# A planned order for VectorE's chains, weight conversions held behind a chain, and one product group in eight products

## The chip, the core and the metric

One core of a Trainium2 chip runs the whole program: TensorE (PE, with its weight loads PEld), VectorE (DVE), ScalarE (ACT), GpSimd (POOL) and SyncE (SP), the last two mostly issuing DMA. The metric is the device time of one execution in microseconds. Before the change the median of three executions is 723.2 us (722.88 to 724.81).

## The reference, cut to what matters

A gated recurrence with complex gates per head, then a dense block with squared relu:

```python
mag = np.sqrt(a_re * a_re + a_im * a_im)
scale = np.minimum(mag, 0.999) / (mag + 1e-06)
a_re_n, a_im_n = (a_re * scale, a_im * scale)
for t in range(S):                      # S = 768; batch 4, 8 heads, head_dim 48
    new_re = ar * S_re - ai * S_im
    new_im = ar * S_im + ai * S_re
    kv = np.einsum('bhd,bhe->bhde', k[:, :, t], v[:, :, t])
    S_re, S_im = (new_re + kv, new_im)
    y[:, :, t] = np.einsum('bhd,bhde->bhe', q[:, :, t], S_re)
...
h = x @ w_in                            # x: 3072 x 384, w_in: 384 x 2048
r = np.maximum(h, 0.0)
return ((r * r) @ w_out).astype(np.float32)   # w_out: 2048 x 384
```

## The kernel before, in words

The 3072 rows are worked in six **units** of 512 rows. For each unit there are three stages.

The **chain** (function `chain`) turns the gates of the unit into running products. A unit's heads are held in two halves of four heads (z = 0 and 1, tiles `aq0`, `f0` and `aq1`, `f1`). For each half `roots` and `normalise` bring the gates to the right length: ScalarE does squares, Ln and Exp (L905 to L917), VectorE L901 to L929. `inner` multiplies four neighbouring rows together: three rounds of two products (L948) and two sums (L954, L956), each round needing the one before. TensorE then turns the last products (L981, tile `xn`), ScalarE copies them to `e` (L996 to L1005), and `scan` runs through them on VectorE: a long row of small complex products, each two multiplications and a sum (L1031, L1033, L1035), ending in `xn` (L1094, L1099). That is turned back (L981, L1116). `apply` multiplies the result into the gates (L1165, L1169), takes the magnitude (L1173 to L1185) and forms the products with k and q (L1188, L1197) that the next stage reads; `gather` moves the k products by DMA to the tile `KC` (L1233).

The **pairs** (function `pairs`) work on two heads at a time, four pairs to a unit. In units 0 and 1 TensorE transposes (L1292) and ScalarE copies (L1296, tile `QT`); later units transpose on VectorE and by DMA. TensorE forms the scores (L1310), VectorE masks them (L1313, tile `A`), TensorE forms the states from the gathered tile (L1338), VectorE sums these (L1347, L1349), TensorE multiplies scores and states with v and q (L1362, L1366, bank `yp`), ScalarE copies the result (L1372) and a DMA puts it into `xT`.

The **dense** stage (function `dense`) works a unit in two groups of 256 rows: hidden blocks on TensorE (L1402), relu and square on ScalarE (L1433, L1434), and the projection. Unit 0 projects with the plain product (L1448). Later units use either `eight` (eight products of half size, L1499) or `seven` (seven products with sums of operands made on VectorE at L1514 and sums of results at L1523). The list `SEVEN` says which; before, these are the second groups of units 1 and 2 and both groups of units 3 to 5. The sums of weights that `seven` needs are made at L1489.

The **weights** arrive as 64-bit numbers in 16 pieces, 8 of each matrix, and are converted on the chip: for each piece ScalarE scales the low words (L795), VectorE masks and shifts the high words (L801), carries the top bits (L805) and adds (L808). In a piece that is `mixed` ScalarE does the top bits in another way (L799), and L805 is not there. Pieces 0 to 5 of the first matrix and the last two pieces of the second are not mixed before. Raw pieces wait in tiles that are not yet needed (`raw1`, `raw2`), two of them in the `g` tile and three in the room of the second matrix.

The order of all instructions comes from the class `Plan`. Each step names its engine, an assumed duration, the keys it reads and writes, and a rank. `order` is a list scheduler: of the engine that can start first it takes, among the steps that are ready, the one of lowest rank. Ranks are pairs: matmuls' followers (0, n), pairs (1, n), chain (2, n) with small offsets, conversions (2, 0.3) and (2, 0.6), dense (3, n), checks of the weights (5, ...). A step is ready when its producers are done plus a hop per engine; a producer on the same engine has no hop. The result is written out engine by engine, and each engine runs its list in that order and waits where it must. A step may hold several instructions: two of the recurrence's products, all three of a complex product.

`check` steps are range checks: sums of squares of q, k, v and the gates, and maxima, that decide at the end whether a slower general path has to run. They are ScalarE squares with an accumulated sum (L932, L936, L1138, L1141).

## Time and profile before

| what | value |
|---|---|
| median of three executions | 723.2 us |
| the profiled execution | 726.46 us |
| its span, first to last instruction | 724.7 us |
| granted TensorE clock, mean | 0.985 |
| PE busy | 637.5 us (88%) |
| DVE busy | 555.9 us (77%) |
| ACT busy | 354.9 us (49%) |
| POOL busy | 176.2 us (24%) |
| DMA | 79.51 MB, mean 110 GB/s |

The profile is of one execution. A busy share is a mean over stages with different limits. In unit 0 there is no dense work yet, so TensorE is idle and the chain is seen bare; later units' chains run beside the dense work of the unit before. Names such as `f<-aq` say which tile an instruction writes and which it reads. A row of the timeline gives the start, the duration, the engine, the line, the operation and how many were merged. A wait is put down to what came last. Some matmul records are missing from the trace, so a short hole of TensorE put down to "issue" need not be idle time.

### The profile page before, as it was taken

The page shows a single profiled execution, that of the slowest core. Times are in us where ns is not written, and L with a number is a line of the kernel's source. Part 1 is how long each engine was busy: PE and PEld are TensorE (multiplying, and loading weights), DVE is VectorE, ACT ScalarE, POOL GpSimd, SP SyncE. Part 2 cuts the span into 40 slices and gives each one's busy share as a digit, 9 for nine tenths or more (in the row PEclk, how much of TensorE's full clock was granted, in tenths as well). Part 3 has the DMA queues.
Part 4 walks back from the last instruction along what each step waited for, and adds up shares of the span by engine and source line. Part 5 has one row for each costly group of instructions (what it writes and reads, how often), then busy time and mean ns, then how long its engine had stood idle before and what let it go on. Part 6 is the DMA issues. An engine that isn't in the chain of part 4 may idle for free. (4 is left out here: it accounts for less than half of the span.)

```text
span 724.7 us, 11426 instructions
## 1 busy us (share of the span) xinstructions
PE 637.5 (88%) x4042; PEld 570.8 (79%) x4042; DVE 555.9 (77%) x1125; ACT 354.9 (49%) x588; POOL 176.2 (24%) x334
## 2 busy tenths in 40 slices
PE   0005779999999999986999999999999999999996
PEld 0005668678768998985998898999998989989996
DVE  6999995798878597977796587897887979428721
ACT  6674456958475435324824556535448344032230
POOL 6502427051400003305022432022223033023200
PEclk9999989999999999998999999999999999999998
DMA  9730348530441003456016555016543043358600
GB/s 287 240 125 22 98 107 177 209 66 18 133 129 30 1 23 100 114 158 152 2 30 167 146 124 103 1 33 164 133 147 73 0 120 78 94 191 326 239 2 27
DMA packets 56355, 79.51 MB, mean 110 GB/s; under 512 B 10944, under 2 KB 38464, under 8 KB 56288
## 3 DMA queue, kind: packets, MB, share of 16 engines
q0 software_dynamic: 15232, 40.72, 18.2%
q1 hardware_dynamic: 36928, 32.98, 18.1%
q10 hardware_dynamic: 4128, 4.98, 2.5%
q8 instruction: 34, 0.56, 0.3%
q14 instruction: 33, 0.27, 0.1%
HBM read 48.76 MB, written 4.72 MB: 74 GB/s over the span
## 5 line engine op out<-in xcount | busy, mean ns | idle before, releaser
L1402 PE MATMUL d<-xT,w 128*128 128x256 f32 x1056 | 238.4, 383 | 4.9 <-issue 3.5
L1402 PEld LDWEIGHTS d<-xT,w 128*128 128x128 f32 x1056 | 199.5, 191 | 33.7 <-issue 5.9
L1499 PE MATMUL d<-w,g 128*128 128x192 f32 x768 | 131.9, 327 | 0.0
L1499 PEld LDWEIGHTS d<-w,g 128*128 128x128 f32 x768 | 125.2, 190 | 0.7 <-issue 0.4
L1233 POOL DMA_DIRECT2D KC<-f x160 | 79.1, 502 | 154.7 <-DVE f L1197 91.7
L1433 ACT ACTIVATE g<-d 128x512 f32<-128x512 f32 x88 | 52.2, 593 | 106.2 <-PE d L1402 83.9
L1460 POOL DMA_DIRECT2D out_dram<-ot x22 | 12.3, 559 | 244.6 <-DVE ot L1523 184.7
L1499 PE MATMUL d<-T,g 128*128 128x192 f32 x384 | 68.0, 327 | 0.0
L1499 PEld LDWEIGHTS d<-T,g 128*128 128x128 f32 x384 | 62.7, 190 | 0.6 <-issue 0.6
L1434 ACT ACTIVATE g<-g 128x512 f32<-128x512 f32 x96 | 60.5, 631 | 3.0
L1372 ACT COPY yt<-yp 112x512 f32<-112x512 f32 x24 | 26.4, 1101 | 72.0 <-PE yp L1366 66.1
L1514 DVE TENSOR_TENSOR g<-g 128x512 f32<-128x512 f32 x64 | 42.9, 683 | 24.0 <-ACT g L1434 14.0
L875 POOL DMA_DIRECT2D v<-in_v_dram x80 | 46.3, 586 | 48.2 <-ACT ot L1518 19.6
L1310 PE MATMUL sc<-QT 96*128 96x128 f32 x368 | 48.5, 286 | 3.7 <-ACT QT L1296 2.3
L1310 PEld LDWEIGHTS sc<-QT 96*128 96x128 f32 x368 | 44.9, 198 | 6.8 <-ACT QT L1296 3.4
L1165 DVE TENSOR_TENSOR f<-aq,xn 128x384 f32<-128x384 f32 (+1 forms) x64 | 45.4, 751 | 1.4 <-ACT xn L1116 1.3
L1197 DVE TENSOR_TENSOR f<-aq 128x384 f32<-128x384 f32 (+1 forms) x64 | 45.0, 753 | 0.5
L1448 PE MATMUL d<-w,g 128*128 128x384 f32 x128 | 43.6, 488 | 0.0
L1362 PE MATMUL yp<-A,v 128*48 128x128 f32 x320 | 36.1, 299 | 3.7 <-DVE A L1313 3.6
L948 DVE TENSOR_TENSOR f<-aq 128x384 f32<-128x384 f32 x72 | 36.9, 554 | 1.0
L1313 DVE TENSOR_TENSOR A<-sc,mask 128x512 f32<-128x512 f32 x45 | 30.0, 684 | 8.2 <-PE sc L1310 8.0
L1523 DVE TENSOR_TENSOR ot<-ot,d 128x192 f32<-128x192 f32 x64 | 21.7, 349 | 19.0 <-PE d L1499 18.6
(186 smaller groups left out, 944.9 us busy)
## 6 DMA issues: line engine op xcount, KB each, us to landing
QT<-aq SPq DMA_DIRECT2D x128, 64.0 KB, 2.0
f<-in_moe_w_in_dram POOLq DMA_DIRECT2D x8, 768.0 KB, 7.0
f<-in_moe_w_out_dram POOLq DMA_DIRECT2D x8, 768.0 KB, 6.4
KC<-f POOLq DMA_DIRECT2D x104, 48.0 KB, 1.8
out_dram<-ot POOLq DMA_DIRECT2D x22, 192.0 KB, 2.4
QT<-aq ACTq DMA_DIRECT2D x64, 64.0 KB, 2.3
v<-in_v_dram POOLq DMA_DIRECT2D x80, 48.0 KB, 3.5
xT<-yt SPq DMA_DIRECT2D x36, 96.0 KB, 2.4
```

The lines of the kernel that those rows point to most:

```text
L875: lambda i=i, c=c, src=src: pool.dma_start(out=t[32 * c:32 * c + 32, i], in_=src[c]), vrank, 32 * 1536, 4.0,
L948: dve.tensor_tensor(out=f, in0=a[:, :, :, c - 1], in1=a[:, j, :, c].unsqueeze(1).to_broadcast([C, 2, HH, D]), op=ALU.mult)
L1165: lambda j=j, r=r: dve.tensor_tensor(out=f4[:, j, r], in0=a[:, r], in1=over(j), op=ALU.mult), late[z])
L1197: lambda j=j, r=r, o=o: dve.tensor_tensor(out=o[:, :, :, r * D:(r + 1) * D], in0=qk[:, j], in1=a[:, r], op=ALU.mult), late[z])
L1233: lambda i=i, c=c, queue=queue: queue.dma_start(out=kc[32 * c:32 * c + 32, i], in_=nat[32 * i:32 * i + 32, c]),
L1310: pe.matmul(sa[:, j], lhsT=T[:, j, 1, h], rhs=T[:, j, 0, h], start=True, stop=True)
L1402: pe.matmul(ps, lhsT=w1[:, f // FP, m, ts(f % FP, C)], rhs=xT[:, n % 2, m, ts(grp, G)], start=(m == 0), stop=(m == NM - 1))
L1433: act.activation(out=o, in_=ps, func=AF.Relu)
L1434: act.activation(out=o, in_=o, func=AF.Square)
L1448: pe.matmul(ps, lhsT=gt[:, f % 2, ts(i, C)], rhs=w2[:, f], start=(f == 0), stop=(f == NF - 1))
L1499: pe.matmul(bank[b][:, 0:DH], lhsT=g4[:, r, j], rhs=w(j), start=first and j == 0, stop=last and j == NT - 1)
L1514: step("DVE", tt(4 * C), gk(x0, h) + gk(x1, h), gk(o, h), lambda: dve.tensor_tensor(out=g4[:, o, sl], in0=g4[:, x0, sl], in1=g4[:, x1, sl] ...
```

## The change

It changes the planner's rules, cuts steps finer, and moves some work. Line numbers of the new file differ from those of the profile; where rows of the new order are shown, the words beside them give the old line.

- *Distance behind the producer.* A producer on the same engine whose result is read now counts with a hop (`DRAIN`: 0.12 us on VectorE, 0.13 on ScalarE). Steps of several instructions are cut into single ones: the recurrence's products and sums, each complex product of the scan, the copies and sign changes beside it.
- *Holding for the chain.* When the best ready step has a rank of (2, 0.2) or more, which includes conversions, the planner looks ahead (`HOLD`: 0.15 us on VectorE, 0.8 on ScalarE) and takes a step of lower rank that will be ready by then.
- *Unit 0's roots* get a rank ahead of its recurrence.
- *Pairs' products unlinked.* In `apply` the two halves of a complex product get keys of their own, and the product with k is written to a scratch tile in place of over k, so that the steps behind wait for less.
- *Five weight pieces later.* Pieces 3 to 7 of the first matrix are converted behind unit 0's pairs in the plan, held until the recurrence of its second half is done. Pieces 3, 4 and 5 become `mixed`: their three L805 go, three L799 come. The tiles of the raw pieces change places: pieces 1 and 2 now wait in `g`, 3 to 5 in the second matrix's room.
- *Range checks.* One square of the roots now accumulates its own sum in place of a second square; the checks of q, k and v get a rank of (2, n + 0.9), behind the unit's chain.
- *Seven and eight.* The second group of unit 1 uses `eight`.
- Assumed durations on ScalarE: 0.08 us less for each, 0.22 more for one that accumulates.

The core of the diff:

```diff
+    HOLD, URGENT, FILL = {"DVE": 0.15, "ACT": 0.8}, (2, 0.2), (2, 0.2)
+    DRAIN = {"DVE": 0.12, "ACT": 0.13}
...
-                hop = 0.0 if same else self.HOP[steps[d][0]]
+                hop = self.HOP[steps[d][0]]
+                if same:
+                    hop = self.DRAIN.get(e, 0.0) if d in steps[n][7] else 0.0
...
+            if steps[n][4] >= self.FILL and e in self.HOLD:
+                m = min((m for m in wait[e] if at[m] <= t + self.HOLD[e]),
+                        key=lambda m: (steps[m][4], m))
+                if steps[m][4] < self.URGENT:
+                    n, t = m, max(t, at[m])
...
+    SOON = 3
...
-    SEVEN = [(n, grp) for n in range(FAST, NU) for grp in range(n < 3, 2)]
+    SEVEN = [(n, grp) for n in range(FAST, NU) for grp in range(n < 3, 2) if n > 1]
...
-        return n / 1200.0 + 0.18
-
+        return n / 1200.0 + 0.10
+
+    SUM = 0.22
...
+    raw1 = [(KC[1].bitcast(U32), [("KC", 1, 0), ("KC", 1, 1)])] + graw + [w2slot(s) for s in (2, 1, 0)]
...
+        held = [("a", 1)] if SOON <= i < NPIECE else []
...
-        mixed = NPIECE - 2 <= i < 2 * NPIECE - 2
+        mixed = SOON <= i < 2 * NPIECE - 2
...
-        step("DVE", ts2(PW), keys, wk, lambda: dve.tensor_scalar(
+        step("DVE", ts2(PW), keys + held, wk, lambda: dve.tensor_scalar(
...
-        first = (CHAIN, 0.25) if n == 1 else rank
+        first = (CHAIN, 0.25) if n == 1 else (CHAIN, n - 0.02) if n == 0 else rank
...
+            check("ACT", ac(Y) + SUM, key(z, 1), key(z, 3), lambda: act.activation(
+                out=t, in_=f1, func=AF.Square, accum_out=sums[:, n, 2 + z:3 + z]), first)
...
-            check("ACT", ac(Y), key(z, 3), [], lambda: act.activation(
-                out=junk[:, 0:Y], in_=t, func=AF.Square, saturate=False,
-                accum_out=sums[:, n, 2 + z:3 + z]), first)
...
-                step("DVE", 2 * tt(m) + 0.06, [("a", z)], key(z, 0), lambda c=c: terms(c), ahead)
-                step("DVE", 2 * tt(m // 2) + 0.06, key(z, 0), [("a", z)],
-                     lambda c=c: joined(c), ahead)
+                for j in range(2):
+                    step("DVE", tt(m), [("a", z)], [("in", z, j)] + (key(z, 0) if c == 1 else []),
+                         lambda c=c, j=j: dve.tensor_tensor(
+                             out=f[j], in0=a[:, :, :, c - 1],
+                             in1=a[:, j, :, c].unsqueeze(1).to_broadcast([C, 2, HH, D]),
+                             op=ALU.mult), ahead)
+                for r, op in ((0, ALU.subtract), (1, ALU.add)):
+                    step("DVE", tt(m // 2), [("in", z, 0), ("in", z, 1)] + key(z, 0), [("a", z)],
+                         lambda c=c, r=r, op=op: dve.tensor_tensor(
+                             out=a[:, r, :, c], in0=f[0][:, r], in1=f[1][:, 1 - r], op=op), ahead)
...
-            def go():
-                dve.tensor_tensor(out=g1, in0=xx, in1=y(0, 1).to_broadcast(shape),
-                                  op=ALU.mult)
-                dve.tensor_tensor(out=g2, in0=xx[:, ::-1], in1=y(1, 3)[:, ::-1],
-                                  op=ALU.mult)
-                dve.tensor_tensor(out=dst, in0=g1, in1=g2, op=ALU.add)
-            step("DVE", 3 * tt(cnt) + 0.24, reads, writes + (own or K), go, rk)
+            for i, (g, x_, y_) in enumerate(((g1, xx, y(0, 1)), (g2, xx[:, ::-1], y(1, 3)[:, ::-1]))):
+                step("DVE", tt(cnt), reads, [(own, i)],
+                     lambda g=g, x_=x_, y_=y_: dve.tensor_tensor(
+                         out=g, in0=x_, in1=y_.to_broadcast(shape), op=ALU.mult), rk)
+            step("DVE", tt(cnt), [(own, 0), (own, 1)], writes,
+                 lambda: dve.tensor_tensor(out=dst, in0=g1, in1=g2, op=ALU.add), rk)
...
-                check("ACT", ac(Y), [("qk", j)] + [("k", j)] * r, [], lambda r=r: act.activation(
+                check("ACT", ac(Y) + SUM, [("qk", j)], [], lambda r=r: act.activation(
                     out=junk, in_=QK[j][:, ts(r, Y)], func=AF.Square, saturate=False,
-                    accum_out=sums[:, n, 4 + 2 * j + r:5 + 2 * j + r]), late[j])
-            check("ACT", ac(Y), [("v", vs(n))], [], lambda: act.activation(
+                    accum_out=sums[:, n, 4 + 2 * j + r:5 + 2 * j + r]), (CHAIN, n + 0.9))
+            check("ACT", ac(Y) + SUM, [("v", vs(n))], [], lambda: act.activation(
                 out=junk, in_=vv[vs(n)][:, ts(j, Y)], func=AF.Square, saturate=False,
-                accum_out=sums[:, n, 8 + j:9 + j]), late[1])
+                accum_out=sums[:, n, 8 + j:9 + j]), (CHAIN, n + 0.9))
...
-                step("DVE", tt(n1), kf[0] + kf[1], [("a", z)],
+                step("DVE", tt(n1), kf[0] + kf[1] + [("a", z)], [("ap", z, p, r)],
...
-            step("DVE", tt(n1), kf[1] + [("qk", z)], [("k", z)],
+            step("DVE", tt(n1) + 0.06, kf[1] + [("qk", z)], kf[0],
                  lambda: dve.scalar_tensor_tensor(
-                     out=qk[:, 1].rearrange("p h c d -> p (h c d)"), in0=t,
-                     scalar=lv[:, n, 1:2], in1=qk[:, 1].rearrange("p h c d -> p (h c d)"),
+                     out=f0, in0=t, scalar=lv[:, n, 1:2],
+                     in1=qk[:, 1].rearrange("p h c d -> p (h c d)"),
...
-            for i in range(NPIECE):
+            for i in range(SOON):
...
+            for i in range(SOON, NPIECE):
+                convert(i)
```

What this does to the order, at three places. The first is VectorE in unit 0, from the roots to the first recurrence; `f0`, `aq0` are the first half of the heads, `f1`, `aq1` the second. Before:

```order
L919 SCALAR_TENSOR_TENSOR f0_70<-f0_70 128x768
L921 SCALAR_TENSOR_TENSOR f0_70<-f0_70 128x768
L926 SCALAR_TENSOR_TENSOR f0_70<-f0_70 128x768
L929 TENSOR_TENSOR aq0_68<-aq0_68,f0_70 128x1536
L948 TENSOR_TENSOR f0_70<-aq0_68 128x384 x2
L954 TENSOR_TENSOR aq0_68<-f0_70 128x4x48
L956 TENSOR_TENSOR aq0_68<-f0_70 128x4x48
L948 TENSOR_TENSOR f0_70<-aq0_68 128x384 x2
```

The same place now, where L930, L932, L937 and L940 are the old L919, L921, L926 and L929, L957 the old L948 and L963 the old L954 and L956:

```order
L932 SCALAR_TENSOR_TENSOR f0_70<-f0_70 128x768
L937 SCALAR_TENSOR_TENSOR f0_70<-f0_70 128x768
L940 TENSOR_TENSOR aq0_68<-aq0_68,f0_70 128x1536
L930 SCALAR_TENSOR_TENSOR f1_71<-f1_71 128x768
L957 TENSOR_TENSOR f0_70<-aq0_68 128x384
L932 SCALAR_TENSOR_TENSOR f1_71<-f1_71 128x768
L957 TENSOR_TENSOR f0_70<-aq0_68 128x384
L937 SCALAR_TENSOR_TENSOR f1_71<-f1_71 128x768
L963 TENSOR_TENSOR aq0_68<-f0_70 128x4x48
L940 TENSOR_TENSOR aq1_69<-aq1_69,f1_71 128x1536
L963 TENSOR_TENSOR aq0_68<-f0_70 128x4x48
```

Before, one half ran to the end of its recurrence before the other's roots went on. Now the second half's roots stand between the steps of the first half.

The second place is VectorE in unit 0's pairs, between the second half's first and second gather products; `w1` is the first weight matrix. Before:

```order
L1197 TENSOR_TENSOR f1_71<-aq1_69 128x2x4x48 x4
L1169 TENSOR_TENSOR aq1_69<-f1_71 128x384 x2
L805 SCALAR_TENSOR_TENSOR w1_66<-g_95,w1_66 128x768
L808 ISA w1_66<-g_95,w1_66 128x1536
L801 TENSOR_SCALAR w1_66<-xT_92 128x768
L808 ISA w1_66<-xT_92,w1_66 128x1536
L801 TENSOR_SCALAR w1_66<-T_72 128x768
L1313 TENSOR_TENSOR A0_86<-sc0_113,mask_98 128x512
L1176 TENSOR_TENSOR f1_71<-f1_71 128x384
```

Now, where L1340 and L1342 are the old L1347 and L1349, L1167 the old L1176, L1306 the old L1313, L812 the old L801, and L1174 to L1179 the old L1183 to L1188:

```order
L1342 TENSOR_TENSOR S1_85<-tr1_116,St1_89 96x96
L1167 TENSOR_TENSOR f1_71<-f1_71 128x384
L1306 TENSOR_TENSOR A0_86<-sc0_113,mask_98 128x512
L812 TENSOR_SCALAR w1_66<-g_95 128x768
L1306 TENSOR_TENSOR A1_87<-sc1_114,mask_98 128x512
L1174 SCALAR_TENSOR_TENSOR f1_71<-f1_71,lv_99 128x384
L1176 SCALAR_TENSOR_TENSOR f1_71<-f1_71 128x384
L1179 SCALAR_TENSOR_TENSOR f1_71<-f1_71,lv_99,aq1_69 128x384
L1190 TENSOR_TENSOR f1_71<-f1_71,aq1_69 128x2x4x48 x2
```

Of the conversions between the first and the last gather products of unit 0 this one L812 is left; the others stand behind the last products now.

The third place is TensorE where unit 1's pairs begin; `tr` banks take the transposes of the first half's products, and the L1448 rows are the projection of unit 0's second group, two trace records to each call. Before:

```order
L1292 MATMUL tr0_115<-ident_96,f0_70 96x128 x4
L1292 MATMUL tr1_116<-ident_96,f0_70 96x128 x4
L1448 MATMUL d0_110<-w2_67,g_95 128x384 x4
L1292 MATMUL tr0_115<-ident_96,f0_70 96x128 x4
L1292 MATMUL tr1_116<-ident_96,f0_70 96x128 x4
L1448 MATMUL d0_110<-w2_67,g_95 128x384 x2
```

Now, where L1441 is the old L1448 and L1285 the old L1292:

```order
L1441 MATMUL d0_110<-w2_67,g_95 128x384 x16
L1441 MATMUL d1_111<-w2_67,g_95 128x384 x6
L1285 MATMUL tr0_115<-ident_96,f0_70 96x128 x4
L1285 MATMUL tr1_116<-ident_96,f0_70 96x128 x4
L1441 MATMUL d1_111<-w2_67,g_95 128x384 x2
L1285 MATMUL tr0_115<-ident_96,f0_70 96x128 x4
L1285 MATMUL tr1_116<-ident_96,f0_70 96x128 x4
L1441 MATMUL d1_111<-w2_67,g_95 128x384 x2
```

Before, all 32 projection calls of that group stand behind the pairs' first transposes, so between or behind the pairs; now 22 of the 32 stand ahead of them.

110 lines of the change are left out of this document (45 added, 65 removed).

## The prediction

> **What bounds the kernel now.** I read the stretches of the span first, cut where the work changes hands: the first dense matmul that runs on without a break, the first gather products of unit 1, the first dense matmuls after units 1 and 2, the last matmul. Columns: start and end, length, busy time of PE, PEld, DVE, ACT and POOL, the granted TensorE clock, the DMA share, GB/s.
>
> ```profile
> 0.00:112.45 112.45, 43.20 (x321) 37.41 (x321) 99.95 (x208) 62.33 (x99) 40.97 (x86) 0.96 0.49 146
> 40.00:80.00 40.00, 17.53 (x107) 15.83 (x108) 37.42 (x97) 20.99 (x32) 8.15 (x16) 1.00 0.13 39
> 98.85:112.45 13.60, 11.37 (x81) 9.67 (x81) 12.06 (x21) 3.16 (x6) 5.84 (x12) 0.75 0.67 164
> 112.45:172.83 60.38, 60.38 (x255) 47.21 (x254) 46.67 (x111) 49.53 (x82) 21.34 (x36) 1.00 0.48 127
> 172.83:225.10 52.27, 50.98 (x373) 38.93 (x371) 41.00 (x79) 33.84 (x60) 12.90 (x26) 1.00 0.37 103
> 225.10:331.75 106.65, 102.27 (x679) 94.85 (x677) 83.92 (x163) 43.74 (x71) 16.21 (x32) 0.98 0.27 72
> 331.75:718.00 386.25, 380.64 (x2423) 352.42 (x2422) 284.05 (x566) 165.46 (x278) 84.76 (x156) 1.00 0.39 109
> ```
>
> Until 112.45 VectorE is the bound (99.95 of 112.45 us busy, 37.42 of 40 in its densest stretch) and TensorE is mostly idle. After that TensorE is full: 60.38 of 60.38, 50.98 of 52.27, 102.27 of 106.65, 380.64 of 386.25. Next the list of what TensorE waited for after 112 us (total, times, longest):
>
> ```profile
> PE yp L1362 <- DVE A L1313: 3.6, 4, 1.1
> PE d L1402 <- issue: 3.5, 1, 3.5
> PE sc L1310 <- DVE A L1313: 1.3, 1, 1.3
> PE tr L1292 <- ACT QT L1296: 1.3, 1, 1.3
> ```
>
> Only 3.6 + 1.3 = 4.9 us are waits for VectorE's masked scores. So the time is: when unit 0 lets the dense work begin, plus TensorE's work, plus a few us. Two things can pay: an earlier 112.45, and the 4.9 us. But an earlier start pays only while TensorE is fed, and its next food, unit 1's pairs, comes from VectorE and ScalarE.
>
> **The change, part by part.**
>
> *Distance behind the producer.* In unit 0's recurrence (L948 to L956) the timeline gives start, duration, engine, line:
>
> ```profile
> 17.53 0.36 DVE L954 TENSOR_TENSOR aq<-f 128x192 f32<-128x192 f32 x1
> 17.81 0.35 DVE L956 TENSOR_TENSOR aq<-f 128x192 f32<-128x192 f32 x1
> 18.20 1.03 DVE L948 TENSOR_TENSOR f<-aq 128x384 f32<-128x384 f32 x2
> ```
>
> L956 does not need L954 and starts 0.28 us after it, though that takes 0.36. L948 needs L956 and starts 0.39 after it. A dependent neighbour costs 0.11 us. Of the 18 dependent neighbours in unit 0's roots, normalisation and recurrence, the new order (first place in the section on the change) keeps 6 and separates 12: 12 x 0.11 = 1.3 us. The scan behind it is one serial chain and has nothing to put between; only its last two sums gain a distance, 0.2 us. [...]
>
> *Five weight pieces later.* These rows stand around the scan:
>
> ```profile
> 34.84 0.96 DVE L805 SCALAR_TENSOR_TENSOR w<-w,w 128x768 uint32<-128x768 uint32 x1
> 35.84 0.96 DVE L808 CUSTOM_DVE_ANT_0 w<-w,w 128x1536 uint16<-128x1536 uint16 x1
> 36.85 0.36 DVE L1031 TENSOR_TENSOR KC<-e 128x192 f32<-128x192 f32 x1
> 50.32 0.55 DVE L801 TENSOR_SCALAR w<-w 128x768 uint32<-128x768 uint32 x1
> 50.91 0.96 DVE L805 SCALAR_TENSOR_TENSOR w<-w,w 128x768 uint32<-128x768 uint32 x1
> 51.79 1.49 DVE L1165 TENSOR_TENSOR f<-aq,xn 128x384 f32<-128x384 f32 x3
> ```
>
> The L808 at 35.84 goes from ahead of the scan to behind it: -0.9 (35.84 to the memset ahead of 36.85). Behind the scan L801 and L805 took 51.79 - 50.32 = 1.47; now that one L808 of 0.96 stands there: -0.5. Then the long part, from the end of the first gather products to that of the last (62.99 to 98.85), by line L801, L805, L808 and L908, in this order:
>
> ```profile
> 62.99:98.85 35.86, 2.77 (x5) 0.96 0.27 67
> 62.99:98.85 35.86, 2.87 (x3) 0.96 0.27 67
> 62.99:98.85 35.86, 4.79 (x5) 0.96 0.27 67
> 62.99:98.85 35.86, 0.95 (x1) 0.96 0.27 67
> 96.89 1.96 DVE L1197 TENSOR_TENSOR f<-aq 128x384 f32<-128x384 f32 x4
> 112.45 2.18 PE L1402 MATMUL d<-xT,w 128*128 128x256 f32 x8
> ```
>
> Of these 2.77 + 2.87 + 4.79 + 0.95 = 11.4 us one L801 (0.55) stays ahead of the last products (second place): -10.8. From the last products to the dense start, 96.89 to 112.45, conversions and unit 1's roots fill the gaps before and now: 0, between -2 (fewer of unit 1's steps) and +2 (more conversions ahead of the last scores). Sum for the dense start: -1.3 - 0.2 - 0.9 - 0.5 - 10.8 = **-13.7**, so about 98.8.
>
> This is work put off, not removed: of the conversions only three L805 go for good (2.87), against three more ScalarE steps of 1.9 each, which I cost at nothing because ScalarE is busy 62.33 of 112.45 there; without that cover, 1.9 each. One of them now stands between the copy of xn and those of e; VectorE's conversions end no earlier, so it is covered, else it costs 1.2.
>
> *What survives to the end of unit 1's pairs.* Unit 1's second half now starts on ScalarE only behind the relu steps of the seventh dense block (its order has all seven ahead); before it stood in front of them:
>
> ```profile
> 116.08 1.53 ACT L905 ACTIVATE f<-aq 128x1536 f32<-128x1536 f32 x1
> 130.62 0.58 ACT L1433 ACTIVATE g<-tr 128x512 f32<-128x512 f32 x1
> 131.23 0.63 ACT L1434 ACTIVATE g<-g 128x512 f32<-128x512 f32 x1
> 148.64 0.36 DVE L1031 TENSOR_TENSOR KC<-e 128x192 f32<-128x192 f32 x1
> 172.83 1.97 DVE L1197 TENSOR_TENSOR f<-aq 128x384 f32<-128x384 f32 x4
> 225.14 1.13 PE L1402 MATMUL d<-xT,w 128*128 128x256 f32 x4
> ```
>
> The seventh ends 131.86 - 112.45 = 19.4 after the dense start, so at 98.8 + 19.4 = 118.2: 2.1 later than 116.08. In return six relu pairs of 1.24 (7.4 us) no longer stand inside that half's roots. Unit 1's scan (148.64) thus moves by +2.1 to -5.3; I take -1.5, near the middle. The dense gain has shrunk to that, and TensorE has used up its cover. How much, the next rows say:
>
> ```profile
> 132.59 13.06 PE L1448 MATMUL d<-w,g 128*128 128x384 f32 x40
> L1448 PE MATMUL d<-w,g 128*128 128x384 f32 x64 | 22.7, 489 | 0.0
> ```
>
> The second is the group between 172.83 and 225.10. One record is 13.06 / 40 = 0.3265 us; 64 lay among unit 1's pairs, 20 do now (third place; a call is two records). 44 x 0.3265 = 14.4 us leave, so TensorE needs 52.3 - 14.4 = 37.9 there. VectorE needs 41.0, and at its densest rate (37.42 of 40) 43.8: it is the bound, and 52.3 becomes 43.8: -8.5, between 0 and -11.3. With -1.5, dense work on unit 1 starts 10.0 earlier than 225.14.
>
> *One product group by eight instead of seven.* Unit 1's second group leaves the seven-product form. Rows: the end of a chain piece on TensorE, then two VectorE groups.
>
> ```profile
> 465.60 16.90 PE d L1499 x104
> L1514 DVE TENSOR_TENSOR g<-g 128x512 f32<-128x512 f32 x64 | 42.9, 683 | 24.0 <-ACT g L1434 14.0
> L1523 DVE TENSOR_TENSOR ot<-ot,d 128x192 f32<-128x192 f32 x64 | 21.7, 349 | 19.0 <-PE d L1499 18.6
> ```
>
> TensorE gets 16 more records at 16.90 / 104 = 0.1625: **+2.6**, fully on its path. VectorE loses 8 x 0.683 + 3 x 0.349 = 6.5 us in the same stretch as the 4.9 us of waits; I take **-3.5** of them, between 0 and -4.9.
>
> *At nothing:* the checks. A square that now accumulates replaces one of its own; it lies on ScalarE (busy 43.74 of 106.65 and 165.46 of 386.25). From 331.75 on TensorE is full and its work is the same: 0.
>
> Sum: -10.0 - 3.5 + 2.6 = **-10.9**. The profiled execution took 726.46 (span 724.7), the median run 723.2, 3.3 less; I take the difference over to the median: 723.2 - 10.9 = **712.3 us**.
>
> **The rivals.**
>
> *A. All of it survives.* VectorE keeps ahead, TensorE never waits: -13.7 - 4.9 + 2.6 = -16.0, 707.2. For it: 13.7 of the 60.38 us behind 112.45 VectorE was idle. Against it: ScalarE's order, above.
>
> *B. Unit 1's pairs do not get shorter.* Each pair goes through transposes, copies, scores, mask and product, and the chain from pair to pair, not VectorE's load, may set the 52.3: -1.5 - 3.5 + 2.6 = -2.4, 720.8. For it: TensorE already waited for single copies there (1.3).
>
> *C. The clock falls there.* With the cover gone TensorE works in bursts, as from 98.85 to 112.45, where it was granted 0.75. At that, its 37.9 become 50.5: -1.8 instead of -8.5, so 719.0. The Trainium skill ("TensorE: Matmul & The Clock Gate", section "HAM oscillation — how this bites in real kernels") says the same in general: gaps over some 3.4 us bring the half clock back, each time anew.
>
> *D. Slower: ScalarE's queue blocks.* Checks on unit 2's q and k stand ahead of copies of unit 1's later pairs, and wait for loads:
>
> ```profile
> 201.30 0.84 ACT L1138 ACTIVATE junk<-aq 128x768 fp8e5<-128x768 f32 x1 [2.40 <-DMA aq<-in_k_dram]
> aq<-in_k_dram SPq DMA_DIRECT2D x8, 384.0 KB, 7.2
> ```
>
> Before, one waited 2.40. If unit 1's pairs come earlier and the loads do not, each half can wait a whole load of 7.2: 14.4 on the pairs, 43.8 becomes 58.2. Sum: -10.9 + 14.4 = +3.5, 726.7. It decides from 10.9 us of such waits on.
>
> [...]
>
> **How the numbers follow.** Forecast 0.42, A 0.17, B 0.16, C 0.12, D 0.08, E 0.05. A measurement of this kernel can tell about 0.3% (2.2 us) from no change. Forecast, A, C and E are faster; B lies at the bound, half to each side; D is slower: faster 0.84, same 0.08, slower 0.08. The range runs from A, less the bound of 2 on the dense start and less 2 of the waits that A leaves (703), to B (721); D and the tails are left out.
>
> **What would show it.** Right: the dense matmuls run on from 97 to 101 us; between the first and the last gather products of unit 0 VectorE shows one conversion step; unit 1's scan starts at 143 to 151; its pairs take 41 to 47 us with TensorE waiting in them; next to no TensorE wait for masked scores in unit 2. Wrong: a dense start after 105, a pairs stretch of over 50 us (B, or C if the clock there is below 0.9), ScalarE waits on q or k loads of over 5 us (D), or new TensorE waits behind 330 us.

## The result and the profile after

The changed kernel took 705.4 us (median of 4), the kernel before 724.0 beside it (median of 4): a ratio of 0.9699, 95% interval 0.961 to 0.9788. A second measurement of the same kernel, in the experiments below, gave 701.9 against 724.1, 0.9687 (0.965 to 0.9724). The ratios are taken over fast executions alone (of the change's four, the one of 709.6 us is left out), so they are not the quotients of the medians, which lie 18.6 and 22.2 us apart. By the ratios the gain is some 22 us, twice the 10.9 forecast. The profiled execution, 698.23 us with a span of 696.4, is the shortest of that kernel. The steps below are read from it, and they add up to more than the medians do: 724.7 - 696.4 = 28.3 us between the two profiled executions. In the profile of the second measurement (span 700.6) dense work on unit 1 begins at 213.66 instead of 209.63; that is 4.0 of the 4.2 us by which it is longer.

First the stretches of the span after the change, cut at the same events as before: the dense start, unit 1's first gather products, the dense start on unit 1, the last matmul. The second row is the stretch in which the clock had been 0.75. Columns as in the prediction.

```profile
0.00:92.66 92.66, 33.67 (x320) 29.73 (x321) 84.26 (x189) 66.34 (x101) 39.75 (x84) 1.00 0.55 169
98.85:112.45 13.60, 13.60 (x65) 11.97 (x64) 9.39 (x19) 9.56 (x15) 7.39 (x10) 1.00 1.10 248
92.66:166.37 73.71, 73.68 (x300) 55.41 (x299) 58.72 (x131) 50.63 (x87) 23.97 (x39) 1.00 0.44 115
166.37:209.63 43.26, 38.90 (x328) 31.29 (x326) 38.88 (x76) 29.30 (x52) 12.91 (x26) 1.00 0.44 125
209.63:689.70 480.07, 479.60 (x3116) 447.20 (x3114) 363.08 (x718) 205.22 (x341) 101.36 (x187) 1.00 0.38 104
```

Dense work begins at 92.66 instead of 112.45 (-19.8). Unit 1's pairs take 43.26 instead of 52.27, with 4.4 us in which TensorE is not busy. From the dense start on unit 1 to the last matmul it takes 480.1 instead of 718.00 - 225.14 = 492.9 (-12.8), and TensorE is busy in all but 0.5 of them. So -19.8 at the dense start is -15.5 at unit 1's, and with -12.8 behind it that makes the 28.3. What TensorE waited for after its dense start:

```profile
PE tr L1285 <- ACT QT L1289: 1.6, 2, 1.0
PE sc L1303 <- ACT QT L1289: 1.0, 1, 1.0
PE tr L1285 <- DVE St L1340: 1.0, 1, 1.0
PE yp L1355 <- DVE A L1306: 0.6, 1, 0.6
PE d L1395 <- DMA xT<-yt: 0.4, 1, 0.4
```

That is 4.6 us, nearly all among unit 1's pairs. The masked scores (L1306, before L1313) keep it waiting for 0.6 instead of 4.9, and the wait of 3.5 that stood as "issue" at the dense matmuls is gone.

Next VectorE in unit 0, in the timeline: its recurrence, the scan's first rows, the first and the last gather products, with the one conversion (L812) between them, and the dense start on TensorE.

```profile
26.89 0.63 DVE L963 TENSOR_TENSOR aq<-f 128x192 f32<-128x192 f32 x2
27.56 1.03 DVE L957 TENSOR_TENSOR f<-aq 128x384 f32<-128x384 f32 x2
28.62 0.63 DVE L963 TENSOR_TENSOR aq<-f 128x192 f32<-128x192 f32 x2
...
33.34 0.63 DVE L1036 TENSOR_TENSOR KC<-e 128x192 f32<-128x192 f32 x2
34.00 0.36 DVE L1039 TENSOR_TENSOR e<-KC 128x192 f32<-128x192 f32 x1
...
57.73 1.02 DVE L1190 TENSOR_TENSOR f<-f,aq 128x384 f32<-128x384 f32 x2
...
75.27 0.55 DVE L812 TENSOR_SCALAR w<-g 128x768 uint32<-128x768 uint32 x1
...
79.28 1.03 DVE L1190 TENSOR_TENSOR f<-aq 128x384 f32<-128x384 f32 x2
...
92.66 1.99 PE L1395 MATMUL d<-xT,w 128*128 128x256 f32 x8
```

The recurrence ends at 29.25 (before 31.57), the scan starts at 33.34 (36.85), the first gather products at 57.73 (61.11), and the last end at 80.31 (98.85). From the end of the first to the end of the last it is 80.31 - 59.70 = 20.6 us instead of 35.86.

### The profile page after: what moved, and what is told of

The parts are those of the page before. It is cut to its first block, busy times and chain, and to the rows that moved or that the text cites. A ratio compares the mean times of both kernels' runs of the same rounds, so it can differ in the third digit from the quotient of the medians.

```text
span 696.4 us, 11428 instructions
## 1 busy us (share of the span) xinstructions
PE 625.9 (90%) x4058; PEld 563.6 (81%) x4058; DVE 545.3 (78%) x1111; ACT 351.5 (50%) x580; POOL 178.0 (26%) x334
## 4 chain that ended last, share of the span: by engine, by line
PE 83%; DVE 11%; DMA 2%; issue 1%; SPq 1%; ACT 1%; DVEq 0%; ACTq 0%
PE d L1395 33%; PE d L1492 27%; PE d L1441 6%; PE sc L1303 5%; PE tr L1331 3%; PE yp L1355 3%; PE yp L1359 2%; PE tr L1395 1%; PE sc L1395 1%; DVE f L957 1%; DMA aq<-in_a_im_dram 1%; DVE f L1190 1%; PE tr L985 1%; DVE f L1156 1%; DVE aq L963 1%
## 5 line engine op out<-in xcount | busy, mean ns | idle before, releaser
L1395 PE MATMUL d<-xT,w 128*128 128x256 f32 x1056 | 233.6, 380 | 0.4 <-DMA xT<-yt 0.4
L1492 PE MATMUL d<-w,g 128*128 128x192 f32 x832 | 143.3, 327 | 0.0
L1492 PEld LDWEIGHTS d<-w,g 128*128 128x128 f32 x832 | 135.5, 190 | 0.7 <-issue 0.4
L886 POOL DMA_DIRECT2D v<-in_v_dram x80 | 47.8, 605 | 50.2 <-issue 36.5
L1507 DVE TENSOR_TENSOR g<-g 128x512 f32<-128x512 f32 x56 | 37.8, 685 | 28.7 <-ACT g L1427 21.3
L1492 PE MATMUL d<-T,g 128*128 128x192 f32 x336 | 59.9, 327 | 0.0
L1492 PEld LDWEIGHTS d<-T,g 128*128 128x128 f32 x336 | 54.9, 190 | 0.6 <-issue 0.6
L1303 PE MATMUL sc<-QT 96*128 96x128 f32 x368 | 46.3, 279 | 2.0 <-ACT QT L1289 2.0
L1303 PEld LDWEIGHTS sc<-QT 96*128 96x128 f32 x368 | 43.2, 192 | 4.0 <-ACT QT L1289 2.4
L1441 PE MATMUL d<-w,g 128*128 128x384 f32 x128 | 42.9, 487 | 0.0
L1306 DVE TENSOR_TENSOR A<-sc,mask 128x512 f32<-128x512 f32 x45 | 30.0, 681 | 14.7 <-PE sc L1303 14.6
L957 DVE TENSOR_TENSOR f<-aq 128x384 f32<-128x384 f32 x72 | 37.0, 553 | 0.7
L1441 PEld LDWEIGHTS d<-w,g 128*128 128x128 f32 x128 | 23.8, 190 | 15.4 <-DVE w L819 1.0
L1516 DVE TENSOR_TENSOR ot<-ot,d 128x192 f32<-128x192 f32 x61 | 20.8, 350 | 18.8 <-PE d L1492 17.5
L985 PE MATMUL tr<-perm,xn 128*128 128x128 f32 x36 | 5.9, 300 | 29.4 <-ACT xn L967 29.4
```

The costliest lines, as they stand in the source:

```text
L886: lambda i=i, c=c, src=src: pool.dma_start(out=t[32 * c:32 * c + 32, i], in_=src[c]), vrank, 32 * 1536, 4.0,
L957: lambda c=c, j=j: dve.tensor_tensor(out=f[j], in0=a[:, :, :, c - 1], in1=a[:, j, :, c].unsqueeze(1).to_broadcast([C, 2, HH, D]), op=ALU.m ...
L1303: pe.matmul(sa[:, j], lhsT=T[:, j, 1, h], rhs=T[:, j, 0, h], start=True, stop=True)
L1306: step("DVE", tt(L) + 0.05, [(b,)], [("A", a)], lambda: dve.tensor_tensor(out=As[a].rearrange("p (j t) -> p j t", j=W), in0=sa, in1=mask4, ...
L1395: pe.matmul(ps, lhsT=w1[:, f // FP, m, ts(f % FP, C)], rhs=xT[:, n % 2, m, ts(grp, G)], start=(m == 0), stop=(m == NM - 1))
L1441: pe.matmul(ps, lhsT=gt[:, f % 2, ts(i, C)], rhs=w2[:, f], start=(f == 0), stop=(f == NF - 1))
```

## The experiments

All were timed in rounds with the kernel before on the same chip; ratios are to it, with their 95% interval. "Dense start" is the first dense matmul behind unit 0's last pair, read from each run's timeline, and "the rest" is the span less that. Both are of one profiled execution, which can lie some us from the median of its run (7 for the change's first). For the two kernels of the change the pair is 112.45 + 612.3 before and 92.66 + 603.7 after.

The theories, in the order in which they were formed: 1, the dense start carries the gain, and the five pieces carry the dense start. 2, the waits for masked scores in unit 2, the wait for the transposed y and the lower clock there are one bubble, and the eight form removes it. 3, what matters is that the plan's times are true: the cost behind a producer corrects them. 4, the holding rule carries the gain. 5, small waits bring a lower clock in some executions, and that is the spread. 6, holding keeps conversions out of the holes that the cost opens. 7, the rules need single, unlinked steps to put between. 8, on tied steps the cost counts twice. Each expectation names its rival.

**The parts undone one by one.** The pieces early again:

```diff
-    SOON = 3
+    SOON = 8
-    raw1 = [(KC[1].bitcast(U32), ...)] + graw + [w2slot(s) for s in (2, 1, 0)]
+    raw1 = [(KC[1].bitcast(U32), ...)] + [w2slot(s) for s in (2, 1, 0)] + graw
-        mixed = SOON <= i < 2 * NPIECE - 2
+        mixed = NPIECE - 2 <= i < 2 * NPIECE - 2
```

> The changed kernel with the five weight pieces early again (all eight converted ahead of the scan and inside unit 0's pairs, six of them wholly on VectorE, raw tiles in the old order). The rest of the change stays. Theory 1, the dense start carries the gain and the pieces carry the dense start: some 11 to 15 us of conversions stand ahead of unit 0's last products again, the dense matmuls run on from about 105 instead of 92.7, and the time is 12 us above the changed kernel's 704, so about 716, 0.99 of the kernel before. Rival, the planner's distance and the split steps carry the start: dense start below 96, time within 3 us of 704.

Measured: 700.4 us, 0.9661 (0.9632 to 0.9691), dense start 96.75, the rest 602.0. Theory 1 falls: nothing is lost, though the dense start is 3 to 4 us later than in the change (92.7 and 93.4). The stretch from the end of the first gather products to that of the last says why, first with all engines (columns as above), then with VectorE's L818 alone and its L821 alone, the second and third step of a conversion (L814, the first, does not stand in it):

```profile
61.70:85.31 23.61, 21.71 (x200) 20.28 (x200) 22.35 (x50) 13.68 (x24) 14.38 (x31) 0.94 0.43 107
61.70:85.31 23.61, 0.94 (x1) 0.94 0.43 107
61.70:85.31 23.61, 0.96 (x1) 0.94 0.43 107
```

Though all eight pieces may be converted early, only 1.9 us of them stand there (before 10.4, the 11.4 of the prediction less 0.95 of L908, which is a step of unit 1's roots). They are kept out by something else in the change.

The planner's two rules off:

```diff
-    HOLD, URGENT, FILL = {"DVE": 0.15, "ACT": 0.8}, (2, 0.2), (2, 0.2)
-    DRAIN = {"DVE": 0.12, "ACT": 0.13}
+    HOLD, URGENT, FILL = {}, (2, 0.2), (2, 0.2)
+    DRAIN = {}
```

> The changed kernel with the planner's two new rules off (no distance counted behind a producer on the same engine, no holding back for a step that is about to be ready); steps split as in the changed kernel. Theory 1 (each dependent neighbour costs 0.11 us, 12 of them in unit 0's roots and recurrence, and some in each apply): dense start 1.5 to 3 us later than 92.7, time 705.5 to 707. [...] Second rival, the rules are most of the gain: over 8 us slower than 704.

Measured: 726.1 us, 1.0031 (1.0007 to 1.0055): the whole gain is gone. The dense start is at 98.81, where the prediction had put it, but the rest takes 625.0. Its list of TensorE's waits behind the dense start, the longest first, and one of them in the timeline:

```profile
PE tr L985 <- DVE xn L1092: 8.3, 5, 2.9
PE tr L1331 <- DVE St L1342: 2.5, 1, 2.5
PE yp L1355 <- DVE A L1306: 1.8, 2, 1.6
PE d L1492 <- DVE g L1507: 1.7, 2, 1.0
PE sc L1303 <- DVE A L1306: 1.5, 1, 1.5
```

```profile
148.41 0.55 PE L985 MATMUL tr<-ident,xn 128*128 128x128 f32 x3 [2.92 <-DVE xn L1092]
```

TensorE's transposes of xn stand in its list ahead of the time at which VectorE's scan is done; after the change the same row starts at 153.64 and waits for nothing. The five waits for xn are one in each of the units 1 to 5. A start that comes 13.6 us earlier is lost to small waits in every unit, on work whose place in the list was planned too early. The diff shows why it was: the tied complex product of the kernel before was booked with three operations and 0.24 us, twice the 0.12; the split one is booked with the three operations alone. Without the cost behind a producer the plan thus books VectorE's chain shorter than the kernel before did.

Unit 1's second group in seven products again, and the eight products alone on the kernel before (the same line the other way):

```diff
-    SEVEN = [(n, grp) for n in range(FAST, NU) for grp in range(n < 3, 2) if n > 1]
+    SEVEN = [(n, grp) for n in range(FAST, NU) for grp in range(n < 3, 2)]
```

> The changed kernel with unit 1's second group back in the seven-product form. Theory 2, the seven form's extra VectorE work (6.5 us) is what made masked scores late in unit 2: TensorE waits for masked scores there return (3 to 5 us), with the wait for the transposed y behind them (3.5) and a clock below 1.00 near 310 to 330; TensorE has 2.6 less work; sum +4 to +7, 708 to 711. Rival, the earlier start already gave VectorE the lead and the eight form only costs: no waits, 2.6 less, 701.

> The kernel before with only unit 1's second group moved from seven products to eight. By the prediction on record: +2.6 on TensorE, -3.5 of the 4.9 us of waits for masked scores, sum -0.9, 723. Theory 2: the waits (4.9), the wait for the transposed y at 334.6 (3.5) and the lower clock around them (324 to 345, about 3 to 4) are one bubble and go together: -11 to -12 + 2.6 = about -9, 715. Rival: the waits stay and only the cost shows, +2.6, 726.

Measured: seven kept 706.2, 0.9733 (0.9689 to 0.9778); no wait for masked scores behind the dense start on unit 1, one of 2.4 for the transposed y. Its interval overlaps that of the change: neither the cost nor the use of the eight form can be told there. Eight alone 721.7, 0.9962 (0.9938 to 0.9987): on the old order it is worth 0.9 to 4.5 us, with 0.8 of the waits for masked scores and 2.7 of the wait for the transposed y left. Theory 2, that all of it is one bubble that the eight form removes, falls. On the old order the masked scores' part of the prediction is borne out (4.9 to 0.8, where -3.5 was taken); its sum for this part, -0.9, stands at the edge of the interval. The dense start of this run is at 115.6, later than before: in its profile the granted clock is 0.50 from 90 to 106, where the kernel before has 0.79 and 0.78, so the later start may be the clock's.

The pieces alone on the kernel before, which is the first diff the other way round with the conversions of pieces 3 to 7 behind unit 0's pairs:

> The kernel before with only the five weight pieces later (three early ones, the other five behind unit 0's pairs, six of them mixed, the new order of raw tiles). By the prediction on record: dense start 112.45 - 0.9 - 0.5 - 10.8 = about 100, and -8.5 to -10 at the end: 714. Theory 1 in its first form: -13 to -19, 705 to 711. Rival, what is gained at the start is lost in unit 1, whose steps are still tied and whose planner is the old one: within 3 us of 723.8.

Measured: 718.0, 0.9899 (0.9865 to 0.9932), dense start 104.1, the rest 612.3 as before. So by themselves the pieces are worth some 7 us, half of what theory 1 and three quarters of what the prediction gave them; beside the rules no gain of theirs shows (700.4 with them undone).

The checks at their old rank, and the pairs' products linked again:

```diff
-                    accum_out=sums[:, n, 4 + 2 * j + r:5 + 2 * j + r]), (CHAIN, n + 0.9))
+                    accum_out=sums[:, n, 4 + 2 * j + r:5 + 2 * j + r]), late[j])
```

```diff
-                step("DVE", tt(n1), kf[0] + kf[1] + [("a", z)], [("ap", z, p, r)],
+                step("DVE", tt(n1), kf[0] + kf[1], [("ap", z, p, r), ("a", z)],
-            step("DVE", tt(n1) + 0.06, kf[1] + [("qk", z)], kf[0],
+            step("DVE", tt(n1) + 0.06, kf[1] + [("qk", z)], kf[0] + [("k", z)],
...
```

> The changed kernel with the range checks of q, k and v back at their old rank, among the steps of their pairs. By the prediction on record the checks' place is worth 0, so within 2 us of the changed kernel, 700 to 706. Rival, on ScalarE they stand ahead of the squares and copies of unit 0's and unit 1's pairs, six of 0.84 and their reads a unit, some 6 us: 706 to 710.

> The changed kernel with the pairs' products linked again: the second pair of a half waits for the first one's products (through the scaled k and the applied a). Theory 7: with fewer free steps the rules find less to put between in the pairs; 2 to 6 us above the changed kernel, 704 to 710. Rival, what is pulled apart lies in the recurrence and the scan, not in the pairs: within 1.5 us, 701 to 705.

Measured: 704.6, 0.9756 (0.9719 to 0.9793), and 704.5, 0.9743 (0.9717 to 0.9768). The medians lie between the two of the change, the ratios just above, with overlapping intervals; what either costs, if anything, is not settled. The change itself again, and the rules with the split steps alone (pieces early and seven products, by the two diffs above):

> The changed kernel itself once more, for its spread. Its four executions so far: 698.2 at a mean granted clock of 0.998, the others 704.8 to 709.6 at 0.987 to 0.992. Theory 5, small TensorE waits in unit 1's pairs (4.6 us in all, around 190 to 206) bring a lower clock in some executions, and that is the whole spread: a profile at 0.987 to 0.992 shows the same waits, and slices below 0.90 behind them, worth 4 to 8 us. Rival, the order of work differs by waits elsewhere: other waits of over 3 us.

> The changed kernel with the five pieces early again and unit 1's second group back in the seven-product form: what is left are the two rules of the planner, the split steps and the checks' places. Theory 3: the rules carry nearly all, 698 to 706, TensorE with 2.6 us less work than in the run with the pieces early alone (700.4). Rival, the eight form is needed for the waits in unit 2: 705 to 712.

Measured: 701.9 (0.9687) and 701.65, 0.9687 (0.9648 to 0.9726). Without the pieces and the eight form the whole gain is there. What that run keeps beside the rules and the split steps are the unlinked products and the checks' places, undone above without a clear loss, and the rank of unit 0's roots and ScalarE's assumed durations, which no run undoes. With all of these and without the rules the time is 726.1, so the rules are needed; that they and the split steps alone are enough is likely, not shown. The new profile of the change has the same kinds of waits, 5.5 us in all behind its dense start, and one slice behind them with a lower clock:

```profile
185.00:200.00 15.00, 11.74 (x111) 9.99 (x109) 13.41 (x23) 10.95 (x21) 3.52 (x7) 1.00 0.29 71
200.00:215.00 15.00, 13.21 (x110) 11.30 (x111) 11.13 (x24) 10.27 (x17) 0.00 (x0) 0.89 0.39 117
```

That is 0.11 x 15 = 1.6 us of the 4.2 by which its span is longer than that of the first profile (700.6 and 696.4), so theory 5 is borne out in its direction but not shown to be all of the spread; an execution at 0.987 to 0.992, of which it spoke, has no profile (this one has 0.996).

**The two rules taken apart.** The holding off, the cost off, and the cost charged to the plan's clock but unseen when the next step is chosen (without and with holding):

```diff
-    HOLD, URGENT, FILL = {"DVE": 0.15, "ACT": 0.8}, (2, 0.2), (2, 0.2)
+    HOLD, URGENT, FILL = {}, (2, 0.2), (2, 0.2)
```

```diff
-    DRAIN = {"DVE": 0.12, "ACT": 0.13}
+    DRAIN = {}
```

```diff
-                    hop = self.DRAIN.get(e, 0.0) if d in steps[n][7] else 0.0
+                    hop = 0.0
...
+            if prev.get(e) in steps[n][7]:
+                t += self.DRAIN.get(e, 0.0)
+            prev[e] = n
             start[n] = t
```

> The changed kernel with the holding rule off (DVE 0.15, ACT 0.8) and the cost of 0.12 and 0.13 behind a producer kept. Theory 3, without that cost the plan's times run ahead of VectorE's real ones, TensorE's steps are put in an order that waits in every unit, and with it they are right again: the small waits of the run without both rules (23 us between 120 and 720) go, dense start near 99, time 704 to 710. Theory 4, the holding rule is what carries the gain: 718 to 726.

> The changed kernel with the holding rule kept and the cost of 0.12 and 0.13 behind a producer set to nothing. Theory 3: TensorE's small waits in every unit stay, so 718 to 726, though the dense start is at 94 to 96. Theory 4: 700 to 706, the waits gone.

> The changed kernel with the holding rule off, and the 0.12 and 0.13 charged to the plan's clock when a step stands right behind its producer, but unseen by the choice of the next step: the plan's times are right, no distance is sought. Theory 3 (it is the plan's times that matter): within 3 us of the run with the cost alone, 704 to 711. Rival, the distance itself saves the time on VectorE (0.11 us per neighbour pulled apart): slower than that run by as much as the neighbours that come together again, 5 us or more, 712 to 722.

> The changed kernel with the holding rule kept, and the 0.12 and 0.13 charged to the plan's clock when a step stands right behind its producer but unseen by the choice of the next step. Theory 3 (the plan's times matter, the distance itself hardly): no neighbours are pulled apart on purpose, holes do not arise that need holding; some 2 to 4 us above the changed kernel, 706 to 710. Rival, distance and holding together are the gain: like the run with neither, 718 to 726.

Measured, with the run without both rules and the change for comparison:

| cost behind a producer | holding | us, ratio | dense start + the rest |
|---|---|---|---|
| none | no | 726.1, 1.0031 | 98.8 + 625.0 |
| none | yes | 723.5, 0.9972 (0.9949 to 0.9995) | 103.2 + 615.4 |
| in the plan's clock alone | no | 714.3, 0.9848 (0.9815 to 0.9881) | 99.1 + 613.3 |
| in the plan's clock alone | yes | 719.4, 0.9937 (0.9905 to 0.9968) | 101.9 + 612.6 |
| seen by the choice too | no | 712.4, 0.9817 (0.9783 to 0.9851) | 110.1 + 601.6 |
| seen by the choice too | yes | 705.4 and 701.9, 0.9699 and 0.9687 | 92.7 + 603.7 and 93.4 + 607.2 |

Theory 3 holds for half. With the cost in the plan's clock and no distance sought, 12 of the 22 us come back, and this is what its list of waits behind the dense start is:

```profile
PE d L1398 <- DMA xT<-yt: 6.6, 4, 2.8
PE d L1398 <- issue: 4.0, 1, 4.0
```

TensorE no longer waits there for a step of VectorE, as it should if the plan's times are true. The other half needs the distance and the holding together: each without the other gives no time that adds to this (712.4 and 719.4 against 714.3). Theory 3 had the dense starts wrong too: near 99 for the cost alone, where 110.1 was measured, and 94 to 96 for the holding alone, where it was 103.2. With the cost seen and no holding the rest is as short as after the change (601.6); what is lost is lost at the start. The timeline of the run with the cost and no holding shows why, in unit 0's scan:

```profile
38.54 0.62 DVE L1036 TENSOR_TENSOR KC<-e 128x192 f32<-128x192 f32 x2
39.08 0.95 DVE L819 CUSTOM_DVE_ANT_0 w<-w,w 128x1536 uint16<-128x1536 uint16 x1
39.95 0.35 DVE L1039 TENSOR_TENSOR e<-KC 128x192 f32<-128x192 f32 x1
40.22 0.55 DVE L812 TENSOR_SCALAR w<-w 128x768 uint32<-128x768 uint32 x1
40.69 0.62 DVE L1036 TENSOR_TENSOR KC<-e 128x192 f32<-128x192 f32 x2
41.23 0.95 DVE L819 CUSTOM_DVE_ANT_0 w<-w,w 128x1536 uint16<-128x1536 uint16 x1
```

In the plan a scan step is ready 0.12 after its producer, and a conversion is ready now: so conversions of 0.55 and 0.95 fill holes of 0.12, and the chain comes late (dense start 110.1). Holding for 0.15 forbids just that: in the change L1039 follows L1036 at 34.00, 0.66 behind its start. Whether ScalarE's part of the rule is needed:

```diff
-    HOLD, URGENT, FILL = {"DVE": 0.15, "ACT": 0.8}, (2, 0.2), (2, 0.2)
+    HOLD, URGENT, FILL = {"DVE": 0.15}, (2, 0.2), (2, 0.2)
```

> The changed kernel with the holding rule on VectorE alone (0.15), not on ScalarE (0.8). Theory 6, what the rule does is to keep conversions of 0.55 to 0.96 us out of the 0.12 us holes that the cost behind a producer leaves on VectorE: dense start 92 to 96 and 700 to 708, as with both. Rival, ScalarE's part carries it: dense start near 110 and 710 to 714, as without the rule.

Measured: 702.6, 0.9693 (0.9659 to 0.9728), dense start 95.9. Theory 6 holds; no gain from ScalarE's part shows. Why holding costs 5 us where the cost is only in the plan's clock is open.

**The rules on the old tied steps.** The new `Plan` class in the kernel before, with both rules, with the cost alone and with the holding alone:

> The kernel before with only the planner of the changed one (the cost behind a producer, the holding rule); the chain's operations stay tied in compound steps of two to three, whose durations already hold the distance inside them. Theory 7, the rules need something to put between: with compound steps there is little, so at most a third of the gain, 716 to 724. Rival, the rules alone are enough: 702 to 708.

> The kernel before with only the cost of 0.12 and 0.13 behind a producer on the same engine, no holding, steps tied as before. Theory 8, the cost is counted twice there (the tied steps' durations already hold it inside) and the plan's order shifts: most of the 30 us, 740 to 755. Rival, the holding does it: within 6 us of 724.

> The kernel before with only the holding rule (0.15 on VectorE, 0.8 on ScalarE), no cost behind a producer, steps tied as before. Theory 8: within 6 us of 724. Rival, the holding leaves VectorE and ScalarE waiting for chain steps with nothing between: most of the 30 us, 740 to 755.

Measured: both 753.8, 1.0423 (1.0389 to 1.0458), dense start 104.3 and the rest 643.8; the cost alone 738.9, 1.0194 (1.0152 to 1.0236); the holding alone 734.1, 1.0132 (1.01 to 1.0163). Neither theory had this: the same rules that gain 22 us on split steps lose 30 on tied ones, and each alone loses 10 to 14. Theory 7 and its rival had gains; of theory 8's two ranges the first (740 to 755) is just missed, and the holding alone lies between its "within 6 us" and its rival's 740. TensorE's waits in the run with both are long ones behind the pairs and for masked scores:

```profile
PE d L1412 <- DMA xT<-yt: 8.7, 5, 3.9
PE yp L1372 <- DVE A L1323: 4.0, 6, 1.0
PE tr L1302 <- ACT QT L1306: 3.9, 2, 3.2
PE sc L1320 <- DVE A L1323: 3.8, 2, 2.3
```

That the tied steps' assumed durations already hold the cost (the 0.24 above), so that it counts twice, fits the run with the cost alone; that is argued, not shown. Why the holding alone loses is open. So is whether any new rule would have lost here: these three runs keep the ranks and the assumed ScalarE durations of the kernel before.

## Why the prediction was right and wrong

*What bounds the kernel.* Right: the dense start plus TensorE's work plus its waits. Both halves moved, 112.45 to 92.66 and 612.3 to 603.7. Of the signs named, one conversion step, the length of unit 1's pairs and the missing waits for masked scores in unit 2 came; the dense start (97 to 101) and unit 1's scan (143 to 151) came earlier than their ranges.

*Distance behind the producer, 1.3 + 0.2.* This is the step that failed. By the sum a change without it would still reach 712.3 + 1.5 = 713.8; with both rules off it took 726.1, so what was put at 1.5 is, together with the holding, worth some 22. The term priced the rule by the instructions that it pulls apart in unit 0, and there it is near (first gather products 3.4 us earlier, 2.9 in the sum). But the number is also what the planner believes of VectorE: once the steps are cut, the order on every engine in every unit hangs on it. Without it the same instructions take 726, with it in the plan's clock 714, with distance and holding 702 to 705. And the holding, which is among the changes listed, had no term at all.

*Five weight pieces, -10.8.* What the sum says happened: one L812 of 0.55 stands between the first and the last gather products. But the cause was misplaced: with the pieces early again the time is the same, and all but 1.9 us of their conversions still stand elsewhere; alone they gain 7. Which part of the change keeps them out was not run by itself: in the run with the cost and no holding all pieces are converted ahead of the first gather products, many in the scan's holes; without both rules, 1.9 us of them stand in the stretch too. The stretch shrank by 15.3, not 10.8: VectorE's idle time in it fell from 35.86 - 33.89 = 2.0 to 0.4 (20.16 busy of 20.61 in the row below), and the rest, some 3 us, are mask, state and apply steps that now stand ahead of or behind it, which the sum took as unmoved.

```profile
59.70:80.31 20.61, 19.39 (x188) 17.97 (x189) 20.16 (x46) 14.61 (x25) 12.52 (x26) 1.00 0.44 107
80.31:92.66 12.35, 10.76 (x123) 9.64 (x122) 11.88 (x22) 6.22 (x10) 3.75 (x9) 1.00 0.28 66
```

From there to the dense start it took 12.35 instead of 13.60, -1.3, inside its bounds of 2. The granted clock there is 1.00 now and was 0.75; the sum left that out, and how much of the 1.3 it makes is not settled. So -19.8 stands against -13.7. The kernel without the rules has the forecast start, 98.81, but by luck: its first gather products are at 61.95, no earlier than before, and its stretch from their end to that of the last is 21.9, shorter than the forecast 25.1.

*Unit 1's scan and pairs.* Right for the scan, measured from the dense start; for the pairs right in length, but not in its parts. Its second half starts on ScalarE behind the seventh relu step:

```profile
110.86 0.63 ACT L1427 ACTIVATE g<-g 128x512 f32<-128x512 f32 x1
111.41 1.49 ACT L916 ACTIVATE f<-aq 128x1536 f32<-128x1536 f32 x1
```

That is 18.8 behind the dense start (19.4 said). The scan starts at 140.49, 29.1 later; the sum had 147.1 - 118.2 = 28.9. The pairs take 43.3 (43.8 said), with TensorE waiting in them. But in the stretch, cut as the prediction cut it, 32 records of unit 0's projection (L1441) lie, not 20:

```profile
166.37:209.63 43.26, 10.69 (x32) 5.25 (x30) 1.00 0.44 125
```

TensorE is busy for 38.90 (37.9 said) and VectorE for 38.88 (41.0 said), and of TensorE's waits there 2.6 are for ScalarE's copies (L1289) and 1.6 for VectorE. That VectorE is the bound is not borne out, so the near hit is in part luck; in the second profile the pairs take 213.66 - 168.54 = 45.1. Of the dense gain 4.3 is lost up to the dense start on unit 1 (3.7 said), which begins 15.5 earlier instead of 10.0: the whole difference is the dense start's.

*One product group by eight, +2.6 - 3.5, and the rest 0.* This is the second place that failed: -0.9 was said from there on, -12.8 measured. The waits fall from 3.6 + 3.5 + 1.3 + 0.9 + 0.4 = 9.7 to 0.4, all of them and not 3.5. The 3.5 of "issue" was quoted and left without a price. By the rows around it, it is the trip of y through its transposing DMA: the copy of y starts at 333.15, its last DMA is issued at 334.8, the DMAs there took 2.0 to 3.2 us to land, and the matmuls go on at 338.14. That it was exposed only because the last pairs came late is argued. And the clock, 0.91 from 320 to 360 before, is 1.00 now: at most 0.09 x 40 = 3.6, an estimate, as TensorE was busy for 32.88 of the 40. With +2.6 that is -10.3 of the 12.8; the other 2.5 are not accounted for. The eight form is not needed for this: with seven products kept no wait for masked scores came back, though 2.4 of the wait put down to "issue" did.

*The checks, 0:* within the measurement, as far as it goes (0.9756 against 0.9687 and 0.9699 for the change).

*The rivals.* A, all of it survives, came nearest in number, not in mechanism: 4.3 us of the dense gain are lost, and TensorE waits in unit 1's pairs; only behind 209.63 is it fed throughout. B did not come: the pairs shrank. C did not in the first profile (1.00 from 166 to 210); in the second a slice of 0.89 cost 1.6 us, not 6.7. D did not: ScalarE waited 1.5 us for one load in unit 1's pairs, of the gates and not of q or k. The distance is not worth nothing by itself either, on which the chance E stood: with cost and holding the same, a choice that sees the distance and one that does not differ by 702 to 705 against 719.4, though what else changes in those two orders is in that difference too. The rows of the recurrence, 0.28 between independent neighbours and 0.39 between dependent ones, say the same of single instructions.

## What to carry to other kernels

Where a planner writes the order of all engines, a cost in its model is not worth the time of the instructions it describes but the waits that come from its being wrong: when steps are cut that held such a gap in their assumed durations, the gap must come back into the clock, or other engines' work is placed too early. A cost of 0.1 us that the choice sees opens holes in which a greedy list puts steps of 1 us; pair it with a rule that holds them. And a wait that stands in the profile is priced with what may hang behind it (here, it seems, a transfer and the clock), even where its releaser reads "issue".

## What was not expected of the hardware

The granted clock fell without a long gap. In the kernel before, four waits of 1.34, 1.02, 0.96 and 1.05 us between 319 and 328.5 stand ahead of and in a stretch at 0.82:

```profile
320.55 1.16 PE L1310 MATMUL sc<-QT 96*128 96x128 f32 x8 [1.34 <-DVE A L1313]
323.08 0.31 PE L1362 MATMUL yp<-A,v 128*48 128x128 f32 x1 [1.02 <-DVE A L1313]
327.09 0.39 PE L1362 MATMUL yp<-A,v 128*48 128x128 f32 x2 [0.96 <-DVE A L1313]
328.54 0.45 PE L1362 MATMUL yp<-A,v 128*48 128x128 f32 x1 [1.05 <-DVE A L1313]
```

```profile
324.00:330.00 6.00, 3.98 (x42) 3.36 (x40) 5.81 (x13) 3.06 (x5) 0.51 (x1) 0.82 0.20 56
```

The Trainium skill ("TensorE: Matmul & The Clock Gate", section "HAM oscillation — how this bites in real kernels") ties the lower clock to idle gaps of more than about 3.4 us; none of these is half as long, so here several short ones close together seem to have been enough (from 328 to 330 the granted clock is 0.50). They are not always: after the change unit 1's pairs hold waits of 4.2 us in all, the longest 1.0, at a granted clock of 1.00 throughout.
